# Attention followed by two Strassen-multiplied layers on one core: weight halves loaded in the order in which they are converted, one product with v moved to another bank, two matrix products placed between transposes and products with v

## The chip, the cores and the metric

The kernel runs on one core of one Trainium2 chip, in one launch. What is measured is the device time of one execution in microseconds (us). The profile is of one further execution of the same program; times below that carry a decimal point after the start of the span are read from it, counted from the span's first instruction.

## The reference

```python
def _attn_ref(q, k, v):                      # q, k, v: (2, 12, 448, 64)
    scores = scale * np.matmul(q, k.transpose(0, 1, 3, 2))
    scores = np.where(mask, -1000000000.0, scores)       # causal
    scores = scores - np.max(scores, axis=-1, keepdims=True)
    attn = np.exp(scores)
    attn = attn / (np.sum(attn, axis=-1, keepdims=True) + 1e-09)
    return np.matmul(attn, v).astype(np.float32)

def _moe_ref(x, w_in, w_out):                # x: (896, 768), w_in: (768, 2048)
    h = x @ w_in
    g = np.where(h >= 1, h, np.where(h <= -1, 0.0, (h + 1) ** 2 / 4.0))
    return (g @ w_out).astype(np.float32)

def _moe2_ref(x, w_gate, w_val, w_out, rms_g):           # w_gate, w_val: (768, 1536)
    xn = x / np.sqrt(np.mean(x * x, axis=-1, keepdims=True) + 1e-06) * rms_g
    g = xn @ w_gate
    return (g * (1.0 / (1.0 + np.exp(-g))) * (xn @ w_val) @ w_out).astype(np.float32)
```

The output is `_moe2_ref(_moe_ref(attention rearranged to 896 x 768))`. The weights are float64 in memory.

## The kernel before

**Attention.** The 24 pairs of batch and head are taken two heads at a time, in 12 groups (NG = 12, numbered 0 to 11). A group's scores are made in 112-row chunks (`scores`, L974 on TensorE), masked and reduced on VectorE (L982), turned into exponentials on ScalarE (L991), transposed on TensorE (`transposes`, L1012), copied out of PSUM by ScalarE (L1036) and VectorE (L1038), and multiplied with v on TensorE (`pv`, L1069). The product is divided by the row sums when VectorE copies it out (`xsplit`, L1080). The reciprocal row sums take a way of their own: VectorE (L1047), a DMA into a small row in DRAM (`factor`, L1049), two DMAs that spread it over partitions (`spread`, L1055). The table `PIPE` sets the order of these steps; it is run through once per group, with the steps of up to three groups in one pass. `pv(g)` belongs to the pass of group g+2. Every `pv` writes PSUM bank 7, so `pv(g)` cannot begin before `xsplit(g-1)` has read the bank.

**Layers.** The four matrix products (w_in, w_out, w_gate with w_val, w_out of the second layer) are done with Strassen's seven products on halves. The first, called in1 here, has 8 groups of columns with 7 products each; each product is 9 matmuls of 128x128 by 448 (L651), three k-blocks times three terms of a split into a high and a low part. A product is one unit of the list `units`. The first four units are product 1 of group 0, product 1 of group 1, product 2 of group 0 and product 2 of group 1. Products 1, 2 and 5 take tokens that early attention groups give; product 6, seventh in the list, is the first that takes those of the last three.

**Weights.** A weight matrix half (128 x 1536 words, float64) is loaded by `w_load` (L447, a DMA from SyncE) into one of two staging buffers and turned to float32 by `w_float`: a ScalarE pass over the high words (L479), a VectorE pass over the low words (L492; on some halves ScalarE, L490), a VectorE pass that joins them (L503). For the first two groups of in1 this happens during attention, in two half passes of 384 columns per matrix half. In `group`, the loads are asked for in the order src1, src2; the join asks for src2 first (`for i in (1, 0)`). Splits and sums on the results (L416, L424) go to ScalarE, VectorE or GpSimd.

**Order.** `Plan.run` places every operation on engines' time lines from a table of costs, with random trials from a fixed seed, and emits the instructions in the order found. Two of its inputs matter here: `tail`, the time that it assumes between a DMA's issue and its landing (5.0 us for a wide weight load), and `rel`, the earliest time of a load. A change of any of them can reorder everything behind. An engine's own instructions run in that order. TensorE's follow the order of the calls.

Of the kernel before, what the change touches and what calls it, by code (L numbers as in the profile page):

```python
# [27 lines left out]
PART = (0.1, 0.3, 1.0, 0.05)  # L28
GUARD = 0.0
BUSY = 7  # L30
QUIET = (5.0, 7.0)
JITTER = 0.5

# [66 lines left out]
class Plan:  # L100
# [104 lines left out]
    def place(self, peat, jitter, cross, same=0.06, guard=0.4):  # L205
# [23 lines left out]
        for i in order:  # L229
            best = None  # L230
            for e, (d, shared) in self.alts[i].items():
# [18 lines left out]
                else:  # L250
                    moved = True
                    while moved:
                        moved = False
                        for line, m in both:
# [4 lines left out]
                            while k < len(line) and line[k][0] < t + d + m:  # L259
                                t = max(t, line[k][1] + m)  # L260
                                moved = True
                                k += 1
                if e == "POOL" and best and any(peat[q] + lag - QUIET[0] < t + d and t < peat[q] + lag + QUIET[1]
                                                for q in self.quiet[1:]):
# [32 lines left out]
MM = 0.2035  # L297
GLEADS = ((24, 18, 16), (24, 18, 16), (24, 18, 16))
MOST1 = 2
AHEAD = 2  # L300
INTO = {2: 11, 21: 21, 22: 22, 3: 12}
FIRST = (21,)
# [8 lines left out]
def kernel(  # L311
# [43 lines left out]
    def ap(b, dtype=None):  # L355
        t = b.space.tile[:, b.off:b.off + b.n]
        return t if dtype is None else t.bitcast(dtype)
# [22 lines left out]
    def bank(i):  # L380
        return pst[:, i, :S]

    def bk(i):
        return BANK + i
# [23 lines left out]
    early = [True]  # L408
# [32 lines left out]
    def w_load(src, rel=0.0, most=3, area=None):  # L441
        if staged[0] >= min(staged[1], most):
            raise NoSpace
        st = SF.first(2 * NK * P if wide else NK * P, *((area,) if area else (SHORT, ())))
        staged[0] += 1
        if wide:
            op({"SP": 0.45}, lambda e: nc.sync.dma_start(out=ap(st, I32), in_=src.bitcast(I32)), [], [st],  # L447
               tail=5.0, rel=rel)
        else:
            op({"SP": 0.1}, lambda e: nc.sync.dma_start(out=ap(st), in_=src), [], [st], tail=4.6, rel=rel)  # L450
        return st
# [73 lines left out]
    def prep(stream, need, lead, fn, slow=False):  # L525

        def at(fn=fn, no=stage_no[0]):
            stage[0] = no
            fn()
        preps.append([need - lead, len(preps), need, at, stream, slow])  # L530
# [6 lines left out]
    def group(src1, src2, T, out, need, seeded, ps, rel=(0.0, 0.0), leads=(16, 10, 8)):  # L537
        st, wf, W = {}, {}, {}
        st_id = object()
        first = min(need.values())  # L540
        ld, lc, lm = leads

        def load(i, src):
            def f():
                st[i] = w_load(src, rel[i])
            return f

        def conv(i):
# [3 lines left out]
        def conv_half(i, h):  # L552
# [2 lines left out]
                    wf[i] = SF.first(NK * P, SHORT, ())  # L555
                w_float(st[i], False, wf[i], h)
            return f
        prep(st_id, first, ld, load(0, src1))
        prep(st_id, first, ld, load(1, src2))
        if ps:  # L560
            prep(st_id, first, lc, conv(1))
        else:
# [137 lines left out]
    def outer(n, load_src, G, out, order, plain=(), leads=(12, 8, 5, 20), apart={}):  # L700
# [61 lines left out]
        for p in phases:  # L762
# [6 lines left out]
            elif p == 6 and 22 in alone:  # L769
                line += seq[:AHEAD] + held_back + seq[AHEAD:]  # L770
            else:
# [10 lines left out]
        def load(i, src):  # L782
            def f():
                st[i] = w_load(src, most=MOST1 if plain else 2, area=area)
            return f
# [128 lines left out]
    NG = B * NP  # L914
# [32 lines left out]
    def seq(eng, dur, fn, r=(), w=(), **kw):  # L947
        plan.first.add(op({eng: dur}, lambda e: fn(), r, w, chain=eng, **kw))
# [14 lines left out]
    sbank, tbank, xbank = {}, {}, {}  # L963
# [95 lines left out]
    def pv(g):  # L1059
        i = g % 2  # L1060
        PT = PTs[i]
        xbank[g] = xb = 7
        parts = [(0, 1, 1, 3), (0, 11, 0, 1)] + [(kc, 4 * kc, kc, NCH - kc) for kc in range(1, NCH)]
        by_chunk = bank(xb).rearrange("p (i c) -> p c i", c=NCH)

        def fn():
            for n, (kc, blk, o, w) in enumerate(parts):
                for j in range(2):
                    nc.tensor.matmul(by_chunk[D * j:D * (j + 1), o:o + w], lhsT=Vr[i][:C, j, kc, :],  # L1069
                                     rhs=PT[:C, j, blk:blk + w],  # L1070
                                     start=(n == 0), stop=(n == len(parts) - 1), skip_group_check=True)
        seq("PE", 2.04, fn, [pts[i], vraw[i]], [bk(xb)], tail=0.1)
# [295 lines left out]
    def busy():  # L1368
        for _ in range(BUSY):
            nc.tensor.matmul(pst[:, 7, :P], lhsT=ap(ones), rhs=ap(ones), start=True, stop=True, skip_group_check=True)  # L1370
    seq("PE", 0.42 * BUSY, busy, [ones], [bk(7)])
    load_qk(1)
# [77 lines left out]
    def run_unit():  # L1450
        nonlocal nu
        now[0] = nu
        while later and later[0][0] <= nu:
            later.pop(0)[1]()
        emit_preps(nu, nu)
        units[nu]()
        nu += 1

    for g in range(NG + 2):
        early[0] = g < NG - 2  # L1460
        if g == NG:
            reserved.add(6)
        for what in PIPE:
            if what[0] == "R" and g == 0:
                load_qk(3)
            if 0 <= g + what[-1] < NG:
                if g == NG + 1 and what[0] == "PV":
                    run_unit()
                if g != 1 or what not in AHEAD1.values():
                    step(what[:-1], g + what[-1])  # L1470
                if g == 0 and what in AHEAD1:
                    step(AHEAD1[what][:-1], 1)
# [55 lines left out]
```

## Time and profile before

| | |
|---|---|
| median of 3 runs | 544.54 us (542.80, 544.54, 548.94) |
| the profiled execution | 545.35 us |
| its span, first to last instruction | 543.6 us, 1.75 us less |
| TensorE busy in the span | 531.3 us, 98% |
| VectorE, ScalarE, GpSimd | 472.6, 408.6, 152.1 us |
| granted TensorE clock | 1.000 (of 2.4 GHz) |

The span has three parts: attention up to about 88 us, the layers up to about 539 us, the last outputs. A time line row gives start, duration, engine, line, operation, tiles, shape and count, and in brackets how long the engine was idle just before and what ended it.

### The profile page before, as it was taken

Reading aid. Unit: us, or ns where it says so; the run is one execution under the profiler, and the core shown is the slowest. Engines: PE = TensorE matmul, PEld = TensorE weight load, DVE = VectorE, ACT = ScalarE, POOL = GpSimd, SP = SyncE. Lnnn points to the kernel's source line nnn. Section 1 sums busy time; section 2 is a strip of 40 time slices with the busy share of each in tenths; the row PEclk is TensorE's granted clock in tenths of the full one; section 3 lists DMA queues with packets and bytes.
Section 4 is the critical chain, followed back from the end, with each engine's and each line's share of the span. In section 5 each row is a group of like instructions: output and inputs, shape, how many; then the busy total and the mean of one; then the engine's idle time right before and its main releaser. Section 6 shows DMA issues by size and latency. Waiting matters only on the chain. (4 is left out here: it accounts for less than half of the span.)

```text
span 543.6 us, 8572 instructions
## 1 busy us (share of the span) xinstructions
PE 531.3 (98%) x2904; PEld 469.7 (86%) x2904; DVE 472.6 (87%) x939; ACT 408.6 (75%) x870; POOL 152.1 (28%) x148
## 2 busy tenths in 40 slices
PE   8999999999999999999999999999999999999996
PEld 6766767999999997999999889988999999999996
DVE  5898988999998899867579999989987878999992
ACT  6979888589988899855688854879787659667560
POOL 1176661620122311311011221342213003009360
PEclk9999999999999999999999999999999999999999
DMA  7783562334334765553063300655562533211012
GB/s 229 205 237 124 151 158 68 116 117 174 117 117 149 263 227 190 121 106 93 0 192 87 106 0 9 234 189 177 195 212 91 175 116 117 67 50 51 1 51 102
DMA packets 23372, 70.47 MB, mean 130 GB/s; under 512 B 5600, under 2 KB 13280, under 8 KB 23328
## 3 DMA queue, kind: packets, MB, share of 16 engines
q1 hardware_dynamic: 21456, 67.24, 38.1%
q0 software_dynamic: 1728, 2.62, 2.8%
q8 instruction: 23, 0.38, 0.3%
q14 instruction: 21, 0.17, 0.1%
q10 hardware_dynamic: 144, 0.06, 0.0%
HBM read 64.49 MB, written 2.80 MB: 124 GB/s over the span
## 5 line engine op out<-in xcount | busy, mean ns | idle before, releaser
L651 PE MATMUL ps<-sr 128*128 128x448 f32 x1260 | 259.8, 367 | 0.6 <-DVE sr L424 0.5
L651 PEld LDWEIGHTS ps<-sr 128*128 128x128 f32 x1260 | 235.8, 188 | 23.1 <-DVE sr L424 1.4
L746 PE MATMUL ps<-sr 128*128 128x448 f32 x918 | 188.4, 366 | 1.5 <-DVE sf L1124 0.8
L746 PEld LDWEIGHTS ps<-sr 128*128 128x128 f32 x918 | 171.8, 188 | 17.1 <-DVE sf L1124 1.2
L416 ACT CAST sr<-sf 128x384 fp32r<-128x384 f32 (+1 forms) x254 | 129.9, 537 | 58.5 <-DVE sf L424 25.5
L424 POOL TENSOR_TENSOR sr<-sf,sr 128x384 fp32r<-128x384 f32 (+1 forms) x65 | 89.1, 1383 | 228.7 <-ACT sr L416 207.2
L424 DVE TENSOR_TENSOR sr<-sf,sr 128x384 fp32r<-128x384 f32 (+1 forms) x207 | 126.2, 633 | 18.6 <-ACT sr L416 16.7
L424 DVE TENSOR_TENSOR sf<-ps,sf 128x448 f32<-128x448 f32 (+1 forms) x122 | 71.5, 599 | 13.9 <-PE ps L651 11.8
L479 ACT ACTIVATE sf<-sf 128x768 f32<-128x768 f32 (+1 forms) x72 | 63.2, 885 | 6.6 <-DMA sf<-in_w_in 4.0
L424 POOL TENSOR_TENSOR sf<-sf 128x448 f32<-128x448 f32 (+1 forms) x32 | 40.2, 1259 | 72.4 <-DVE sf L424 17.5
L416 ACT CAST sr<-ps 128x384 fp32r<-128x384 f32 (+1 forms) x82 | 38.4, 488 | 20.5 <-DVE ps L424 7.4
L991 ACT ACTIVATE sf<-ps,sf 112x336 f32<-112x336 f32 (+2 forms) x96 | 46.8, 505 | 9.0 <-DVE sf L982 7.5
L424 DVE TENSOR_TENSOR sr<-ps,sr 128x384 fp32r<-128x384 f32 (+1 forms) x82 | 44.8, 559 | 6.7 <-ACT sr L416 6.0
L424 DVE TENSOR_TENSOR sf<-sf 128x448 f32<-128x448 f32 (+1 forms) x73 | 46.3, 655 | 0.9 <-ACT sf L1187 0.5
L982 DVE CUSTOM_DVE_ANT_0 ps<-ps,sf 112x336 f32<-112x336 f32 (+2 forms) x96 | 41.1, 470 | 7.0 <-PE ps L974 6.1
L503 DVE SCALAR_TENSOR_TENSOR sf<-sf 128x768 int32<-128x768 int32 (+1 forms) x46 | 42.0, 918 | 1.7 <-ACT sf L490 0.6
L490 ACT ACTIVATE sf<-sf 128x768 int32<-128x768 uint8 x34 | 30.9, 912 | 0.0
L1012 PE MATMUL ps<-sf 112*112 112x112 f32 x240 | 27.0, 263 | 2.6 <-ACT sf L991 2.6
L503 DVE SCALAR_TENSOR_TENSOR ps<-sf 128x768 int32<-128x768 int32 x26 | 27.8, 1070 | 1.3 <-ACT sf L490 0.6
L416 ACT COPY ps<-ps 128x448 f32<-128x448 f32 x42 | 21.6, 519 | 9.2 <-PE ps L651 7.1
L1012 PEld LDWEIGHTS ps<-sf 112*112 112x112 f32 x240 | 22.9, 134 | 6.5 <-ACT sf L991 3.7
L974 PE MATMUL ps<-sf 64*112 64x336 f32 (+3 forms) x192 | 27.3, 413 | 1.0 <-DMA sf<-in_qT 0.5
(53 smaller groups left out, 348.9 us busy)
## 6 DMA issues: line engine op xcount, KB each, us to landing
sf<-in_w_out SPq DMA_DIRECT2D x28, 768.0 KB, 4.4
sf<-in_w_in SPq DMA_DIRECT2D x16, 768.0 KB, 5.1
sf<-in_w_gate SPq DMA_DIRECT2D x12, 768.0 KB, 4.3
sf<-in_w_val SPq DMA_DIRECT2D x12, 768.0 KB, 4.4
sf<-in_kT SPq DMA_DIRECT2D x12, 224.0 KB, 3.8
sf<-in_v SPq DMA_DIRECT2D x12, 224.0 KB, 3.6
sf<-row SPq DMA_DIRECT2D x24, 112.0 KB, 4.0
out_T<-sf SPq DMA_DIRECT2D x12, 224.0 KB, 1.9
```

The source lines that it names most:

```text
L416: op(alts, lambda e: nc.scalar.copy(dst, src) if e == "ACT" else nc.gpsimd.tensor_copy(dst, src), r, w, **kw)
L424: op(alts, lambda e: E[e].tensor_tensor(out=dst, in0=a, in1=b, op=alu), r, w, **kw)
L479: lambda e, words=words: nc.scalar.activation(words(1, F32), words(1, F32), ACTF.Prelu, scale=2.0 ** -112, alpha=-2.0 ** 32), [part], [top])
L490: nc.scalar.activation(words(0, I32), byte, ACTF.Copy, scale=7.49 / 255)
L503: nc.vector.scalar_tensor_tensor(out=out, in0=hi, scalar=3, in1=lo, op0=ALU.logical_shift_left, op1=ALU.bitwise_or)
L651: nc.tensor.matmul(bank(o), lhsT=ap(d.sub(x * HW + k * P, P)), rhs=ap(t.sub(y * S, S)), start=(begin and k == 0 and i == 0), stop=(k == HK ...
L746: nc.tensor.matmul(bank(o), lhsT=ap(a.sub(x * HW + d * P, P)), rhs=ap(t.sub(y * S, S)), start=((p == 1 or p > 7) and i0 == 0 and i == 0), ...
L974: nc.tensor.matmul(pst[:C, bs[j], o:o + (c + 1) * C], lhsT=ap(q)[r, c * C:(c + 1) * C], rhs=ap(k)[r, :(c + 1) * C], start=True, stop=True, ...
L982: seq("DVE", 0.145 + 0.00093 * (c + 1) * C, lambda t=t, c=c: nc.vector.tensor_tensor_reduce(out=t, in0=t, in1=ap(mask)[:C, S - (c + 1) * C ...
L991: seq("ACT", 0.23 + 0.0009 * w, lambda c=c, o=o, w=w: nc.scalar.activation(Pn[:C, j, poff[c]:poff[c] + w], pst[:C, sbank[n][j], o:o + w], ...
L1012: nc.tensor.transpose(pst[:C, bs[j][0], o:o + C], Pn[:C, j, poff[c] + kc * C:poff[c] + (kc + 1) * C], ap(ident)[:C, :C])
```

## The change

1. `load` gives the first load's earliest time to the half that is used first, and the two loads of a group that is not `ps` (the first two groups of in1) are asked for in the order src2, src1.
2. While `early[0]` is true (attention passes up to group 9), the plan assumes 8.5 us (WAIT0) in place of 5.0 us between issue and landing of a weight load.
3. `pv(NG - 2)`, the product with v of group 10, writes bank 6 (OWN) instead of bank 7.
4. One unit of in1 is run ahead of `pv(10)` and one ahead of `pv(11)` (FRONT); before, one was run ahead of `pv(11)` only.

```diff
+OWN = 6
+FRONT = (1, 1)
...
+WAIT0 = 8.5
...
-               tail=5.0, rel=rel)
+               tail=WAIT0 if early[0] else 5.0, rel=rel)
...
-                st[i] = w_load(src, rel[i])
+                st[i] = w_load(src, rel[i if ps else 1 - i])
...
-        prep(st_id, first, ld, load(0, src1))
-        prep(st_id, first, ld, load(1, src2))
+        for i, src in ((0, src1), (1, src2))[::1 if ps else -1]:
+            prep(st_id, first, ld, load(i, src))
...
-        xbank[g] = xb = 7
+        xbank[g] = xb = OWN if g == NG - 2 else 7
...
-                if g == NG + 1 and what[0] == "PV":
-                    run_unit()
+                if g >= NG and what[0] == "PV":
+                    for _ in range(FRONT[g - NG]):
+                        run_unit()
```

Lines of the changed kernel are numbered three higher from L447 on (L479 is L482, L651 is L654, L1069 is L1072), a few behind `pv` more. In the rows below, `sf` and `sr` are the two SBUF areas, `ps` is PSUM, `row_64` and `row_65` the two DRAM rows.

ScalarE early in attention (the pass from 15.5 us on), before: two half conversions (L479) stand in one pass.

```order
L1036 COPY sf<-ps 112x4x112 x2
L479 ACTIVATE sf<-sf 128x384
L991 ACTIVATE sf<-ps,sf 112x448 x2
L991 ACTIVATE sf<-ps,sf 112x336
L991 ACTIVATE sf<-ps,sf 112x112
L479 ACTIVATE sf<-sf 128x384
L991 ACTIVATE sf<-ps,sf 112x336
L991 ACTIVATE sf<-ps,sf 112x112
L991 ACTIVATE sf<-ps,sf 112x224
```

The same place in the changed kernel, up to the next conversion.

```order
L1039 COPY sf<-ps 112x4x112 x2
L482 ACTIVATE sf<-sf 128x384
L994 ACTIVATE sf<-ps,sf 112x448 x2
L994 ACTIVATE sf<-ps,sf 112x336
L994 ACTIVATE sf<-ps,sf 112x112
L994 ACTIVATE sf<-ps,sf 112x336
L994 ACTIVATE sf<-ps,sf 112x112
L994 ACTIVATE sf<-ps,sf 112x224
L1039 COPY sf<-ps 112x4x112
L994 ACTIVATE sf<-ps,sf 112x224
L1039 COPY sf<-ps 112x4x112 x2
L482 ACTIVATE sf<-sf 128x384
```

The second conversion moved to the next pass, and so did each of the six behind it; the eighth stands one pass behind the place of the last one before. VectorE's passes that join the words (L503) keep their places, one pass each.

TensorE at the end of attention, before: the 20 transposes of group 11, `pv(10)`, its last 4 transposes, one product of in1, the first matmuls of `pv(11)`.

```order
L1012 MATMUL ps<-sf 112x112 x20
L1069 MATMUL ps<-sf 64x3x112 x2
L1069 MATMUL ps<-sf 64x112 x2
L1069 MATMUL ps<-sf 64x3x112 x2
L1069 MATMUL ps<-sf 64x2x112 x2
L1069 MATMUL ps<-sf 64x112 x2
L1012 MATMUL ps<-sf 112x112 x4
L651 MATMUL ps<-sr 128x448 x9
L1069 MATMUL ps<-sf 64x3x112 x2
```

The same place in the changed kernel.

```order
L1015 MATMUL ps<-sf 112x112 x20
L654 MATMUL ps<-sr 128x448 x9
L1072 MATMUL ps<-sf 64x3x112 x2
L1072 MATMUL ps<-sf 64x112 x2
L1072 MATMUL ps<-sf 64x3x112 x2
L1072 MATMUL ps<-sf 64x2x112 x2
L1072 MATMUL ps<-sf 64x112 x2
L1015 MATMUL ps<-sf 112x112 x4
L654 MATMUL ps<-sr 128x448 x9
L1072 MATMUL ps<-sf 64x3x112 x2
```

A product of 9 matmuls now stands ahead of each of the last two products with v.

VectorE at the same place, before: `xsplit(9)`, two copies out of the transposes (L1038) with the reciprocal and three operations on tokens (L424) between them, `xsplit(10)`.

```order
L1080 TENSOR_TENSOR sf<-ps,sf 128x448
L1038 COPY sf<-ps 112x4x112
L1047 RECIPROCAL sf<-sf 112x8
L424 TENSOR_TENSOR sf<-sf 128x448 x2
L424 TENSOR_TENSOR sr<-sf,sr 128x448
L1038 COPY sf<-ps 112x2x2x112
L1080 TENSOR_TENSOR sf<-ps,sf 128x448
```

The same place in the changed kernel.

```order
L1083 TENSOR_TENSOR sf<-ps,sf 128x448
L1041 COPY sf<-ps 112x4x112
L1050 RECIPROCAL sf<-sf 112x8
L427 TENSOR_TENSOR sf<-sf 128x448 x2
L427 TENSOR_TENSOR sr<-sf,sr 128x448 x3
L1041 COPY sf<-ps 112x2x2x112
L1083 TENSOR_TENSOR sf<-ps,sf 128x448
```

Two more token operations stand ahead of the last copy of transposes, which `pv(11)` needs. On SyncE's queue the first load of group 2 of in1 moved about three passes forward, from behind the v load of group 10 to just ahead of the row write of an earlier group.

## Rows read from the trace of the kernel before

**Rows 1.** The page: busy time, share, instructions; 40 slices; TensorE's clock.
```profile
PE 531.3 (98%) x2904; PEld 469.7 (86%) x2904; DVE 472.6 (87%) x939; ACT 408.6 (75%) x870; POOL 152.1 (28%) x148
PE   8999999999999999999999999999999999999996
PEclk9999999999999999999999999999999999999999
```
**Rows 2.** Time line of PE, attention: first scores of a group, and one wait.
```profile
27.88 2.15 PE L974 MATMUL ps<-sf 64*112 64x448 f32 x16
...
34.06 2.15 PE L974 MATMUL ps<-sf 64*112 64x448 f32 x16
...
40.09 1.45 PE L1012 MATMUL ps<-sf 112*112 112x112 f32 x12 [1.32 <-ACT sf L991]
...
42.34 2.16 PE L974 MATMUL ps<-sf 64*112 64x448 f32 x16
...
49.08 2.39 PE L974 MATMUL ps<-sf 64*112 64x448 f32 x16 [0.49 <-DVE sf L1038]
...
55.62 2.39 PE L974 MATMUL ps<-sf 64*112 64x448 f32 x16
...
62.04 2.15 PE L974 MATMUL ps<-sf 64*112 64x448 f32 x16
...
68.22 2.15 PE L974 MATMUL ps<-sf 64*112 64x448 f32 x16
```
**Rows 3.** Time line of ACT: conversions of the first weights, one with a wait.
```profile
16.81 0.70 ACT L479 ACTIVATE sf<-sf 128x384 f32<-128x384 f32 x1
...
19.68 0.59 ACT L479 ACTIVATE sf<-sf 128x384 f32<-128x384 f32 x1
...
38.23 0.57 ACT L479 ACTIVATE sf<-sf 128x384 f32<-128x384 f32 x1 [2.67 <-DMA sf<-in_w_in]
```
**Rows 4.** Time line of SP's queue: weight loads three and four; spread of group 9.
```profile
23.32 0.46 SPq L447 DMA_DIRECT2D sf<-in_w_in  x1
...
29.57 0.46 SPq L447 DMA_DIRECT2D sf<-in_w_in  x1
...
73.25 0.35 SPq L447 DMA_DIRECT2D sf<-in_w_in  x1
73.65 1.09 SPq L1055 DMA_DIRECT2D sf<-row  x2
```
**Rows 5.** Line L447 up to 100 us: landing of the weight loads.
```profile
DMA to landing us min/median/max: 5.0/6.2/8.6
```
**Rows 6.** Time line of all engines, 38.5 to 48.5: two joins of words, one GpSimd operation.
```profile
38.79 0.56 DVE L503 SCALAR_TENSOR_TENSOR sf<-sf 128x384 int32<-128x384 int32 x1
...
46.93 1.14 POOL L424 TENSOR_TENSOR sr<-sf,sr 128x448 fp32r<-128x448 f32 x1
...
47.11 1.38 DVE L503 SCALAR_TENSOR_TENSOR sf<-sf 128x384 int32<-128x384 int32 x1
```
**Rows 7.** Time line, end of attention: pv(10), pv(11), their waits, and xsplit(9), xsplit(10).
```profile
80.58 0.62 DVE L1080 TENSOR_TENSOR sf<-ps,sf 128x448 f32<-128x448 f32 x1 [0.36 <-DMA sf<-row]
...
81.25 2.11 PE L1069 MATMUL ps<-sf 112*64 112x336 f32 x20 [0.61 <-DVE sf L1080]
...
83.66 2.10 PE L651 MATMUL ps<-sr 128*128 128x448 f32 x9
...
85.80 0.62 DVE L1080 TENSOR_TENSOR sf<-ps,sf 128x448 f32<-128x448 f32 x1 [1.24 <-DMA sf<-row]
...
86.53 2.11 PE L1069 MATMUL ps<-sf 112*64 112x336 f32 x20 [0.77 <-ACT sf L416]
```
**Rows 8.** Time line of PE behind 90 us: the three rows that have a wait.
```profile
207.41 73.18 PE L746 MATMUL ps<-sr 128*128 128x448 f32 x357 [0.79 <-DVE sf L1124]
...
299.98 5.32 PE L746 MATMUL ps<-sr 128*128 128x448 f32 x24 [0.65 <-ACT sr L416]
...
325.52 137.30 PE L651 MATMUL ps<-sr 128*128 128x448 f32 x671 [0.46 <-DVE sr L424]
```

## The prediction, made before the changed kernel was run

> **What bounds the kernel now.** First the page: TensorE is busy 531.3 of 543.6 us at the full granted clock, while VectorE has 87% and ScalarE 75% [rows 1]. No edit shortens a matmul or takes one away, so all that can be won is time in which TensorE stands: 12.3 us over the span, the ends included. So the question goes to TensorE's time line: where is it late, and what ended the wait?
>
> In attention, the first scores of a group (L974) mark one pass. Undisturbed passes take 6.18 us, with a weight conversion in them (27.88 to 34.06) or without (62.04 to 68.22) [rows 2]. Four passes in a row do not: 34.06 to 42.34 is 8.28, then 6.74, 6.54 and 6.42. Over 6.18 that is 2.10 + 0.56 + 0.36 + 0.24 = **3.26 us**. The listed waits show less of it (1.32 at 40.09, 0.49 at 49.08), since matmuls that trickle in with short gaps are drawn as longer ones: the distance between passes is the better measure.
>
> ScalarE's line says where this starts: a conversion begins at 38.23 after 2.67 us idle, ended by a DMA of w_in [rows 3]. So ScalarE asked at 35.56. The fourth weight load was issued at 29.57 [rows 4]; to 38.2 that is 8.6 us, the longest landing of those up to 100 us [rows 5]. ScalarE runs in order: the exponentials behind the conversion, and with them the transposes (1.32 us at 40.09), had to wait for weights that nobody needs before in1 begins at 83.66 [rows 7]. The passes behind are the echo. VectorE's join of weight words takes 0.56 us at 38.79, but 1.38 us at 47.11, where it overlaps a GpSimd operation begun at 46.93 [rows 6]; 0.49 us of wait for VectorE follows at 49.08.
>
> At the end of attention `pv(10)` stands 0.61 us for `xsplit(9)`, which itself waited for the spread row sums; `pv(11)` stands 0.77 us [rows 7]. The view names a ScalarE copy for the latter, but `pv(11)` must also wait for `xsplit(10)` to read bank 7; that ran from 85.80 to 86.42, 0.11 us before `pv(11)`, and had itself waited 1.24 us for its row. I take it to be the releaser. Behind 90 us three waits are left, 0.79 + 0.65 + 0.46 = 1.90 us [rows 8].
>
> **The change part by part.**
>
> *Order of loads, and WAIT0.* Either should end the wait alone. What group 1 needs first is now the third load, issued at 23.32 [rows 4]; with the longest landing it is there at 31.9. WAIT0 also moves the second and all later conversions one pass back (16.81 stays, the one at 19.68 goes to the next pass), so it is asked for near 35.56 + 6.18 = 41.7: 9.8 us of room. The other half, in place at 38.2, is used two passes after that. Price: the eight half conversions of about 0.6 us remain, one per pass; passes of that kind took 6.18. Before, ScalarE's conversions ran a pass ahead of VectorE's joins; now the fourth, near 16.81 + 3 x 6.18 = 35.35, is followed by its join at 38.79 in the same pass, 2.8 us behind its end. That cover is enough; were it gone, VectorE would stand, and at most the 0.6 us of a conversion would show in a pass. Term: **-3.26 us**, between -2.10 (the pass with the wait alone, if the echo has a cause of its own) and -3.26.
>
> The Trainium skill, page "DMA: Bandwidth & Descriptors", section "Anatomy of one DMA — SWDGE (gpsimd) path", gives a DMA about 2.0 us plus its bytes at 436 GB/s: an estimate of 3.8 us for this load of 768 KB. By it the fourth load would have been in place at 33.4, ScalarE would not have stood, and this edit would be worth nothing (545.35 - 1.38 = 543.97). The trace disagrees: 8.6 us and a wait of 2.67.
>
> *The load of group 2 that moved.* On SyncE's queue the weight load that stood just ahead of the spread of group 9 (73.25, then 73.65 [rows 4]) goes about three passes forward, ahead of a row write. The spread behind it cost `xsplit` 0.36 and `pv` 0.61 us at its old place. At the new one the same could happen once: 0 to +0.61. I take 0, since the third load stands four transfers ahead of the spread of a group, as this one will, and the pass from 27.88 to 34.06 has its 6.18 us. Its first VectorE pass now falls into the last pass of attention, where VectorE idled 0.36 us ahead of `xsplit(9)`; no more than a few tenths, on an engine that TensorE then does not wait for.
>
> *Bank 6 and the two products.* `pv(10)` no longer needs `xsplit(9)`: its 0.61 us go. `pv(11)` needs `xsplit(9)` instead of `xsplit(10)`, done 5 us before: its 0.77 us go. A product ahead of each costs nothing, since the same work leaves the row behind; each is 2.10 us of cover [rows 7]. What comes last then is the copy of the last transposes, which `pv(11)` reads: two more token operations stand ahead of it on VectorE, 2 x 0.62 (by `xsplit`, same shape) = 1.24 us, and 0.62 for itself, together 1.86, under the 2.10 of the product that now stands between. Should ScalarE's casts, which feed those operations, be late too, a part of 0.77 comes back: 0 to +0.5, I take 0. Behind `pv(11)` four products instead of five stand before product 6, which needs the last tokens: at 137.30 / 671 = 0.205 us a matmul [rows 8], 4 x 9 x 0.205 = 7.4 us for `xsplit` and three token operations of 0.62, 2.5 us and their handovers. Enough. Term: **-1.38 us**.
>
> *All that stands behind.* The plan is drawn anew, so that 450 us of order on VectorE, ScalarE and GpSimd differ in detail. The work is the same, and before it left TensorE 1.90 us of waits. A new draw can lose them or have as many again: -1.9 to +1.9. I take 0, having no row that favours either.
>
> **Sum.** 545.35 - 3.26 - 1.38 = 540.71 us against the profiled execution. That one lay 0.81 over the median of the three runs; from the median the same terms give 539.90. I take the middle, **540.3 us**, 0.8% under the median.
>
> **The rivals.**
>
> *The layers come out better.* The new draw loses the three waits: 540.3 - 1.9 = 538.4. For it: each is a hand-over at a change of stage, 0.46 to 0.79 us. Against: those changes of stage are still there. *Or worse*, by as much again, perhaps with a late row at the load's new place: 542.2 to 542.8.
>
> *The wait for weights is not in the plain runs.* Landings up to 100 us go from 5.0 to 8.6 us [rows 5]; one of 5.0 would have brought the fourth load by 34.6, ahead of 35.56, with no wait. If runs without the profiler are like that, then the load order and WAIT0 gain nothing there, and 544.54 - 1.38 = 543.2. For it: the lowest of the three runs, 542.80, lies where 545.35 - 3.26 = 542.1 would. Against: the median does not.
>
> *Slower.* The place is the layers, the mechanism VectorE and GpSimd meeting: the join at 47.11 took 0.82 us more beside a GpSimd operation, and TensorE stood 0.49 us behind it [rows 2, 6]. A redrawn order that has them meet, unseen by the plan once real times drift, pays that each time. It decides from 4.64 / 0.49, about ten such meetings that reach TensorE, and takes 21 to be 1% slower; then the time is 545 to 550. For it: the change redraws 450 us. Against: in the same 450 us of before only three waits reached TensorE at all.
> The Trainium skill, page "SBUF — State Buffer", section "Who interferes with whom", says that a VectorE instruction with two SBUF inputs and a GpSimd instruction that reads SBUF exclude each other for the whole instruction. The two joins agree, 1.38 against 0.56 us; by that rule a meeting can cost up to the whole 1.14 us of the GpSimd operation, and four or five would do.
>
> **How the numbers follow.** Forecast 0.50; better layers 0.17; worse layers 0.15; no wait in plain runs 0.12; slower 0.06. The range goes from 538.3 (better layers) to 543.2 (worse layers and the case without a wait); outside are the slow case and tails, under 2 in 10. About 1%, 5.4 us, is what a measurement of this kernel can tell from no change: below 539.1 lie the better layers and about a fifth of the forecast, 0.28; above 550 lies half of the slow case, 0.03; the rest, 0.69, is within.
>
> **What would show it.** In the changed profile: the conversions of L482 without a wait for w_in; first scores 6.18 us apart all through, so that those of 68.22 come at 65.0; joins at 0.56 us; `pv(10)` and `pv(11)` without a wait, the latter over by about 85.8 and both first products of in1 with it; before, `pv(11)` and the second of them, 2.05 and 1.84 us, took from 86.53 to 90.4. The forecast is wrong if a pass stays at 6.5 or more, if rows of sums land late near 55 to 65 us, if a product waits at 85 to 95 us for tokens, or if waits behind 90 us add up to over 4 us.

## The result, and the profile after

The changed kernel takes 548.02 us (median of 21 runs, 545.84 to 553.88), the kernel before 542.95 (21 runs, 541.07 to 548.94): ratio 1.0095, interval 1.0078 to 1.0111. It is slower by 5.1 us (4.2 to 6.0), not faster by 0.8%, and lies outside the range. The profiled execution of the changed kernel took 548.02 us too, its span 546.3.

The page of the changed kernel: busy time, TensorE in 40 slices, its clock.

```profile
PE 533.2 (98%) x2904; PEld 471.7 (86%) x2904; DVE 474.7 (87%) x937; ACT 408.8 (75%) x873; POOL 143.1 (26%) x147
...
PE   8999999999999998999999899999999999999996
...
PEclk9999999999999999999999799999999999999999
```

The sums hardly differ from [rows 1]; the slices do: TensorE has two new gaps, in the slices from 205 and from 300 us, and a lower clock in the second. Attention comes first. The time line of PE, first scores of a group (L977, L974 before), then the end of attention (L654 is a product of in1, L1072 a product with v):

```profile
33.58 2.15 PE L977 MATMUL ps<-sf 64*112 64x448 f32 x16
...
39.76 2.20 PE L977 MATMUL ps<-sf 64*112 64x448 f32 x16
...
46.54 2.39 PE L977 MATMUL ps<-sf 64*112 64x448 f32 x16 [0.48 <-DVE sf L1041]
...
53.13 2.38 PE L977 MATMUL ps<-sf 64*112 64x448 f32 x16
...
59.54 2.15 PE L977 MATMUL ps<-sf 64*112 64x448 f32 x16
...
77.94 2.09 PE L654 MATMUL ps<-sr 128*128 128x448 f32 x9
79.96 2.11 PE L1072 MATMUL ps<-sf 112*64 112x336 f32 x20
...
82.37 2.10 PE L654 MATMUL ps<-sr 128*128 128x448 f32 x9
84.39 2.11 PE L1072 MATMUL ps<-sf 112*64 112x336 f32 x20
86.44 3.91 PE L654 MATMUL ps<-sr 128*128 128x448 f32 x18
```

The pass of 8.28 us [rows 2] is gone (33.58 to 39.76 is 6.18), but the three behind it stay long: 6.78, 6.59, 6.41, against 6.74, 6.54 and 6.42 before. pv(10) and pv(11) have no wait. The third product of in1 starts at 86.44, where before it started near 90.5: 4.1 us, of which 0.45 is an earlier start of the first passes.

Then the gain goes. Both traces hold 2904 matmuls, so the k-th from the end can be compared. The 160 that ran from 181.25 to 215.46 us before, the end of in1 and the start of out1, took 34.2 us; now they take 38.6, from 176.41 to 214.96. The 160 around the norm (295.30 to 327.49 before) took 32.2 and now take 34.9. Behind 330 us both run alike, 2.4 us apart there and 2.7 at the end. The waits of PE behind attention, from its time line:

```profile
161.87 20.58 PE L654 MATMUL ps<-sr 128*128 128x448 f32 x99 [0.39 <-ACT ps L419]
...
183.11 3.91 PE L654 MATMUL ps<-sr 128*128 128x448 f32 x18 [0.66 <-DVE sf L427]
...
199.34 1.69 PE L749 MATMUL ps<-sr 128*128 128x448 f32 x7 [0.93 <-DVE sr L427]
...
205.95 2.70 PE L749 MATMUL ps<-sr 128*128 128x448 f32 x12 [0.91 <-DVE sf L1127]
...
214.04 66.18 PE L749 MATMUL ps<-sr 128*128 128x448 f32 x323 [0.48 <-DVE sr L427]
...
306.89 0.95 PE L1220 MATMUL ps<-sf 128*112 128x1 f32 x8 [1.21 <-DVE sf L427]
308.03 1.65 PE L1220 MATMUL ps<-sf 128*112 128x1 f32 x8 [0.20 <-ACT sf L1190]
```

Where the stretch had one wait of 0.79 before [rows 8] it now has six: 0.66 at the end of in1 and five at out1, 2.8 us in all, three of them shown. That is 2.6 us more; the rest of the 4.4 is matmuls that trickle in. All but two small ones (0.29 and 0.16, ScalarE) end with VectorE, and no wait of TensorE, VectorE or ScalarE in the stretch ends with GpSimd. VectorE's time line there, with GpSimd's (time line of all engines, rows of these two):

```profile
189.93 1.95 POOL L427 TENSOR_TENSOR sr<-sf,sr 128x448 fp32r<-128x448 f32 x1 [1.47 <-ACT sr L419]
190.78 1.52 DVE L495 TENSOR_SCALAR sf<-sf 128x768 int32<-128x768 int32 x1
...
194.14 0.55 DVE L495 TENSOR_SCALAR sf<-sf 128x768 int32<-128x768 int32 x1
...
196.92 1.41 POOL L427 TENSOR_TENSOR sr<-sf,sr 128x448 fp32r<-128x448 f32 x1 [5.04 <-ACT sr L419]
197.24 1.58 DVE L427 TENSOR_TENSOR sr<-sf,sr 128x448 fp32r<-128x448 f32 x1
...
202.28 2.26 POOL L427 TENSOR_TENSOR sr<-sf,sr 128x384 fp32r<-128x384 f32 x2 [3.95 <-ACT sr L419]
...
203.53 1.83 DVE L506 SCALAR_TENSOR_TENSOR sf<-sf 128x768 int32<-128x768 int32 x1
```

The same shift takes 0.55 us at 194.14 and 1.52 at 190.78, where GpSimd's subtraction began 0.85 us before it. Such an overlap of a VectorE operation with a GpSimd operation that reads SBUF, with the VectorE one over 0.25 us longer than others of its shape, is called a meeting from here on. From 182 to 206 us VectorE loses 4.2 us in five meetings (0.41, 0.96, 0.97, 0.97, 0.88 over the usual time of each shape); there it is full (9.8 of the 10 us from 190 on; 9.7 before). The kernel before lost 1.75 in two, at 188.85 and 203.68. Its time line, first a meeting and then a place without one:

```profile
188.51 1.44 POOL L424 TENSOR_TENSOR sr<-sf,sr 128x448 fp32r<-128x448 f32 x1 [1.35 <-ACT sr L416]
188.85 1.58 DVE L424 TENSOR_TENSOR sr<-sf,sr 128x448 fp32r<-128x448 f32 x1
...
194.84 0.62 DVE L424 TENSOR_TENSOR sr<-sf,sr 128x448 fp32r<-128x448 f32 x1
195.06 1.42 POOL L424 TENSOR_TENSOR sr<-sf,sr 128x448 fp32r<-128x448 f32 x1 [5.11 <-ACT sr L416]
195.48 1.02 DVE L424 TENSOR_TENSOR sr<-ps,sr 128x384 fp32r<-128x384 f32 x2
```

At 188.85 they meet. At 195.06 VectorE was already in its operation (0.62, undisturbed), and the two behind it, which take one operand from PSUM, run beside GpSimd at their usual 1.02.

### The profile page after: what moved, and what is told of

Its sections match the earlier page's. It is cut to its first block, busy times and chain, and to the rows that moved or that the text cites. A ratio compares the mean times of both kernels' runs of the same rounds, so it can differ in the third digit from the quotient of the medians.

```text
span 546.3 us, 8551 instructions
## 1 busy us (share of the span) xinstructions
PE 533.2 (98%) x2904; PEld 471.7 (86%) x2904; DVE 474.7 (87%) x937; ACT 408.8 (75%) x873; POOL 143.1 (26%) x147
## 4 chain that ended last, share of the span: by engine, by line
PE 74%; DVE 16%; ACT 6%; issue 2%; DMA 1%; POOL 0%; DVEq 0%; ACTq 0%; POOLq 0%
PE ps L654 36%; PE ps L749 25%; DVE sr L427 6%; DVE sf L427 5%; PE ps L1072 4%; PE ps L977 4%; PE ps L1015 4%; DVE ps L506 2%; ACT sr L419 2%; DMA sf<-in_w_out 1%; ACT sf L994 1%; DVE sf L506 1%; DVE sf L1127 1%; ACT sf L482 1%; PE ps L1373 1%
## 5 line engine op out<-in xcount | busy, mean ns | idle before, releaser
L654 PE MATMUL ps<-sr 128*128 128x448 f32 x1260 | 260.8, 368 | 1.3 <-DVE sf L427 0.7
L654 PEld LDWEIGHTS ps<-sr 128*128 128x128 f32 x1260 | 237.8, 190 | 22.5 <-DVE sf L427 1.0
L427 DVE TENSOR_TENSOR sr<-sf,sr 128x448 fp32r<-128x448 f32 (+1 forms) x207 | 130.0, 653 | 18.9 <-ACT sr L419 17.5
L427 POOL TENSOR_TENSOR sr<-sf,sr 128x384 fp32r<-128x384 f32 (+1 forms) x65 | 83.6, 1296 | 212.5 <-ACT sr L419 192.9
L482 ACT ACTIVATE sf<-sf 128x768 f32<-128x768 f32 (+1 forms) x72 | 62.9, 880 | 3.1 <-DMA sf<-in_w_val 1.8
L427 POOL TENSOR_TENSOR sf<-sf 128x448 f32<-128x448 f32 (+1 forms) x31 | 36.8, 1190 | 106.7 <-DVE sf L427 59.4
L994 ACT ACTIVATE sf<-ps,sf 112x336 f32<-112x336 f32 (+2 forms) x96 | 46.6, 503 | 8.9 <-DVE sf L985 8.0
L506 DVE SCALAR_TENSOR_TENSOR sf<-sf 128x768 int32<-128x768 int32 (+1 forms) x46 | 43.6, 949 | 2.0 <-ACT sf L482 0.8
L493 ACT ACTIVATE sf<-sf 128x768 int32<-128x768 uint8 x37 | 33.5, 906 | 0.0
L977 PE MATMUL ps<-sf 64*112 64x336 f32 (+3 forms) x192 | 27.0, 410 | 1.4 <-DMA sf<-in_qT 0.8
```

Of the source, the lines that this page charges most:

```text
L427: op(alts, lambda e: E[e].tensor_tensor(out=dst, in0=a, in1=b, op=alu), r, w, **kw)
L482: lambda e, words=words: nc.scalar.activation(words(1, F32), words(1, F32), ACTF.Prelu, scale=2.0 ** -112, alpha=-2.0 ** 32), [part], [top])
L493: nc.scalar.activation(words(0, I32), byte, ACTF.Copy, scale=7.49 / 255)
L506: nc.vector.scalar_tensor_tensor(out=out, in0=hi, scalar=3, in1=lo, op0=ALU.logical_shift_left, op1=ALU.bitwise_or)
L654: nc.tensor.matmul(bank(o), lhsT=ap(d.sub(x * HW + k * P, P)), rhs=ap(t.sub(y * S, S)), start=(begin and k == 0 and i == 0), stop=(k == HK ...
L977: nc.tensor.matmul(pst[:C, bs[j], o:o + (c + 1) * C], lhsT=ap(q)[r, c * C:(c + 1) * C], rhs=ap(k)[r, :(c + 1) * C], start=True, stop=True, ...
```

## The experiments

Theory 1: the layers were ordered anew, and the new order is worse wherever TensorE arrives. Theory 2: VectorE sets the pace at the start of out1, so whatever attention gives is waited out there. Theory 3 is in E3 that the wait and the clock at the norm cost the most, and from E7 on that a part of the change carries the loss by itself. Theory 4, formed after E1 to E4: the loss is VectorE standing beside GpSimd, where VectorE is full.

Several kernels keep an order that was planned for another. Their two last lines of the schedule read

```diff
-    plan.run()
+    for i in ORDER:
+        plan.fn[i](NAMES[ENG[i]])
```

with ORDER and ENG written out as tables at the end of the file.

The table holds what the verdicts rest on, worked out from each trace: the 160 matmuls at the start of out1 and the 160 at the norm (us), the excess of VectorE's operations within the former (us over the usual time of their shape, summed over the meetings, and how many they were), and the measured ratio to the kernel before.

```
                              out1 start   excess     norm    ratio and interval
before (profiled; again)      34.2; 34.1   1.75 (2)   32.2
changed (profiled; again)     38.6; 38.5   4.2 (5)    34.9    1.0095  1.0078-1.0111
E1  before, short attention   34.2         1.75 (2)   32.0    1.0030  0.9999-1.0061
E2  changed, 4.4 us late      37.6         4.2 (5)    33.5    1.0185  1.0142-1.0227
E3  changed, norm later       38.1         4.2 (5)    32.6    1.0087  1.0054-1.0120
E4  changed, middle as before 36.1         1.75 (2)   33.5    1.0142  1.0112-1.0173
E5  changed, zeros            34.3         0          33.4    0.9999  0.9975-1.0024
E6  E1 with zeros             34.1         1.75 (2)   32.2    1.0018  0.9992-1.0045
E7  changed, seed 7           36.6         2.4 (3)    32.0    1.0046  1.0019-1.0073
E8  before, seed 7            36.3         4.6 (5)    31.2    1.0031  0.9999-1.0063
E9  changed, six on VectorE   36.2         0          35.0    1.0058  1.0029-1.0087
E10 E9, norm later            36.7         0          32.5    1.0027  0.9998-1.0056
E11 loads alone               37.7         4.9 (5)    34.1    1.0058  1.0032-1.0083
E12 bank and products alone   36.7         4.1 (5)    30.8    1.0056  1.0027-1.0085
E14 before, seed 6            34.4         0.96 (1)   30.7    1.0003  0.9979-1.0026
E16 changed, seed 6           37.7         4.8 (6)    31.1    1.0045  1.0023-1.0068
```

**E1, a shorter attention before the old order.** Bank 6 for pv(10), and in the ORDER table ScalarE's conversion of 38.23 [rows 3] and the three behind it one pass later.

```diff
-        xbank[g] = xb = 7
+        xbank[g] = xb = 6 if g == NG - 2 else 7
```

> The kernel before with a smaller edit: pv(10) writes bank 6, and the ScalarE conversion that waited at 38.23 us and the three behind it stand one pass later in ScalarE's order. The rest of the order, that of all layers above all, is written out as it was before. It takes 2.1 to 3.3 us (the wait for w_in, with or without its echo) and 0.6 us (pv(10)) out of attention. Theory 1 (the changed kernel lost because its layers were ordered anew): the order is kept, so 2.7 to 3.9 us are kept to the end, ratio to before 0.993 to 0.995. Theory 2 (VectorE is full at the start of out1, so TensorE waits out there whatever attention gives): TensorE reaches out1 2.7 to 3.9 us earlier and at 280 us has at most 1 us left; ratio 0.998 to 1.001.

Ratio 1.003 (0.9999 to 1.0061): theory 1's number fails, and theory 2's (0.998 to 1.001) lies at the interval's edge. The time line of all engines shows where the gain went, not at out1 but at 101.74:

```profile
93.35 2.89 POOL L424 TENSOR_TENSOR sr<-sf,sr 128x448 fp32r<-128x448 f32 x2
93.79 2.93 DVE L424 TENSOR_TENSOR sr<-sf,sr 128x448 fp32r<-128x448 f32 x2
...
97.98 3.17 DVE L424 TENSOR_TENSOR sr<-sf,sr 128x448 fp32r<-128x448 f32 x3
...
98.20 1.26 POOL L424 TENSOR_TENSOR sf<-sf 128x384 f32<-128x384 f32 x1 [1.96 <-PE ps L651]
...
101.74 2.50 PE L651 MATMUL ps<-sr 128*128 128x448 f32 x11 [1.58 <-DVE sf L424]
```

TensorE was 1.6 us ahead of the kernel before at 98.6 and level with it at 115. The three subtractions of 97.98 take 1.55 where nothing meets them (E6). The order was the old one; only real times had shifted, and with them six meetings, 4.5 us, fell between 80 and 100 us, where before there were two, 1.1 us.

**E2, the changed kernel arriving late.**

```diff
         def fn():
+            for _ in range(19 * (g == NG - 1)):
+                nc.tensor.matmul(pst[:, xb, :P], lhsT=ap(ones), rhs=ap(ones), start=True, stop=True,
+                                 skip_group_check=True)
             for n, (kc, blk, o, w) in enumerate(parts):
```

> The changed kernel with 19 idle products of the 128 ones ahead of pv(11), about 4.4 us of TensorE (half of the 0.46 us that each took at the start of the program, at the lower clock), in an order that is else the same. It arrives at out1 when the kernel before does. Theory 1: the order of the layers costs what it costs, 548 + 4.4 = 552 us, ratio to before about 1.017. Theory 2: VectorE sets the pace from 187 to 220 us, the delay is taken up by the waits there: 548 to 549.5 us, ratio 1.009 to 1.012.

Ratio 1.0185: theory 1's number. TensorE reached the place at 181.83 us, 0.6 later than before, and still lost 3.4 us there. So the loss isn't a gain waited out. It weighs less than it looks: VectorE's last work of attention came 4.5 us later as well (91.78 for 87.29).

**E3, the norm later.** AT counts the products between the last of the layer and the norm's steps.

```diff
-    AT = ((3, 5, 3, 7), (1, 2, 2, 4))
+    AT = ((3, 5, 3, 7), (2, 3, 3, 5))
```

> The changed kernel in its own order, but TensorE's pieces of the second half's norm (both sums of squares, then the spread) stand one or two products later. Theory 3 (the wait of 1.21 us at 306.89 and the lower clock behind it cost 4 to 4.5 us, apart from the rest): no wait there, matmuls at 0.20 us instead of 0.37 from 309.6 to 316, the second layer's out starts 3 to 4.4 us earlier, 543.6 to 545 us, ratio 1.001 to 1.004. Rival (the wait moves to the spread, the clock falls all the same): at most 1 us, ratio 1.007 or more.

Split. In the trace the wait of 1.21 us gives way to one of 0.52, the granted clock stays at 1.00 (as in E10, below) and the stretch takes 32.6 instead of 34.9; the times, 1.0087, don't show it.

**E4, the middle as before.** The ORDER table between 100 and 250 us of the plan is the old kernel's, as far as reused buffers allow; some operations had to stand earlier than there.

> The changed kernel, in which the operations of the layers from the end of attention to the end of out1's first three quarters (100 to 250 us of the plan) stand in the order and on the engines of the kernel before; ahead of it and behind it its own. Theory 1: at least 2.5 of the 3.7 us lost from 187 to 220 us come back, 544 to 545.5 us, ratio 1.002 to 1.005. Theory 2: the waits at out1 stay, 547 to 548.5 us, ratio 1.007 to 1.011.

Neither: 1.0142. From 112 to 133 us TensorE lost 3.8 us at four waits for ScalarE and VectorE (0.89, 0.74, 1.34, 0.79) that neither kernel has; that they come from the operations moved ahead isn't shown. Only the stretch at out1 can be read: two meetings as in the old order, but 36.1 us, halfway. So the number of meetings alone doesn't set the loss.

**E5, GpSimd without reading.** Six subtractions are replaced.

```diff
-        op(alts, lambda e: E[e].tensor_tensor(out=dst, in0=a, in1=b, op=alu), r, w, **kw)
+        def fn(e):
+            if now_at[0] in CUT:
+                return nc.gpsimd.memset(dst.bitcast(F32), 0.0)
+            E[e].tensor_tensor(out=dst, in0=a, in1=b, op=alu)
+        op(alts, fn, r, w, **kw)
```

> The changed kernel in its own order, but the six subtractions that GpSimd has from 181.9 to 203.4 us write zeros instead, so that they read nothing (six low halves of operands are left out). Theory 4 (the loss at out1's start is VectorE standing beside GpSimd: five VectorE operations from 183 to 204 us take 0.4 to 1.0 us more than others of their shape, 4.0 in all, where VectorE is full): the excess goes, and the matmuls from 181.25 to 215.46 us of before, which took 34.2 there and 38.6 in the changed kernel, take 34.5 to 36; 544 to 545.5 us, ratio to before 1.002 to 1.005. Theory 1 in its plain form (VectorE's own order is worse there, GpSimd has no part): at most 1 us, ratio 1.007 or more.

Ratio 0.9999, 5.2 us below the changed kernel. Up to 181 us the two traces run alike to 0.04 us; then E5 takes 34.3 instead of 38.6. That is more than theory 4's 34.5 to 36. Another 1.5 us of the gain lies at the norm, which the edit doesn't touch: the wait there is the same, but the lower clock behind it lasted 3.4 us instead of 6.8. VectorE's time line, the same operations as above at 197.24 and 203.53:

```profile
194.79 0.62 DVE L430 TENSOR_TENSOR sr<-sf,sr 128x448 fp32r<-128x448 f32 x1
...
200.12 0.95 DVE L510 SCALAR_TENSOR_TENSOR sf<-sf 128x768 int32<-128x768 int32 x1
```

Theory 4 holds at out1's start, theory 1 in its plain form (VectorE's own order) falls. Since a zero also is there earlier than a difference, E9 was needed.

**E6, E1 without its meetings.** The edit of E5 in E1, for six operations from 80.1 to 99.4 us.

> The first experiment's kernel (attention 1.6 us shorter, lost again by a wait of 1.58 us for VectorE at 101.74), but the six subtractions and additions that GpSimd has from 80.1 to 99.4 us write zeros instead (parts of six operands are left out). Theory 4: VectorE loses the 4.5 us that six of its operations took too long from 80 to 100 us, the wait at 101.74 goes, and TensorE keeps 1.6 us and more to the end; ratio to before 0.995 to 0.998. Theory 2 (what attention gives is waited out in any case): a wait of the same size for VectorE or ScalarE there or at out1, ratio 1.000 to 1.003.

No meeting is left from 80 to 100 us and the wait at 101.74 is gone; TensorE keeps its lead through in1 and out1 (34.1). The ratio, 1.0018 (0.9992 to 1.0045), doesn't show the gain: the mechanism is in the trace, the time stays inconclusive. In the profile the lead of 1.15 us over the kernel before (E13) stands up to 216 us and is gone at 278; between the two lies a stretch in which TensorE runs 2% slower (last section).

**E7, E8, E14, E16, other draws.** Only the seed changes (to 6 in E14 and E16).

```diff
-SEED = 5
+SEED = 7
```

> The changed kernel with another seed of the planner (7 for 5), nothing else. Theories 1 and 4 (a draw of the layers' order decides): the excess of VectorE's operations from 180 to 205 us is another, and the time is 2 us or more from 548, more likely below: ratio to before 0.997 to 1.006. Rival (theory 3, a part of the change itself costs it): within 1 us of the changed kernel, ratio 1.008 to 1.011.

> The kernel before with another seed (7 for 5), nothing else. Theories 1 and 4, if the draw of the kernel before was a good one: more excess on VectorE from 80 to 110 or 180 to 205 us and 2 to 5 us more, ratio 1.004 to 1.009. Rival (draws cost nothing, the change does): ratio 0.998 to 1.002.

> The kernel before with seed 6. Theory 4: every draw but the first has three or four meetings of VectorE and GpSimd from 180 to 200 us; then 3 to 4 here too, 2 to 4 us lost at out1's start, ratio to before 1.002 to 1.008. If the draw of before is ordinary: one meeting, 0.998 to 1.001. Its attention shows a third time whether the wait for w_in comes.

> The changed kernel with seed 6, whose planned time is the shortest of its five seeds. Theory 4: its time goes with the meetings from 180 to 205 us; with three or four of them ratio 1.003 to 1.009, with one or none 0.997 to 1.002 and a version as fast as the kernel before or faster.

A draw is worth 2 to 3 us: the changed kernel goes from 1.0095 to 1.0046 and 1.0045, the one before from 1 to 1.0031 and 1.0003. In these draws the stretch at out1 goes with the meetings (34.1 to 34.4 us with one or two, 36.3 to 38.6 with three or more), but not in proportion: 2.4 us of excess give 36.6 (E7), 4.6 give 36.3 (E8), 4.2 give 38.6. Where meetings are few (E14) the time is that of before. E8 lies between its two expectations. E14's expectation fails: seed 6 has one meeting, so the old order was no rare luck. With seeds 5, 6 and 7 the kernel before has 2, 1 and 5 meetings, the changed one 5, 6 and 3, and with none of the three is the changed kernel the faster.

**E9, E10, the six on VectorE.** In the ENG table six operations change engine; E10 adds E3's edit.

```diff
-    (ENG of operations 1050, 1095, 1097, 1132, 1134, 1145: GpSimd)
+    (VectorE)
```

> The changed kernel in its own order, but the six subtractions that GpSimd has from 181.9 to 203.4 us run on VectorE, at the same place of the order; nothing is left out. Theory 4 counts VectorE's time: 4.0 us of standing beside GpSimd go, six operations of 0.53 us each from start to start come, 3.2 us; so 0.8 us are won at out1's start, with the earlier results at most 2: 546 to 547.5 us, ratio to before 1.006 to 1.009. Rival (GpSimd's results came late, and VectorE's fullness has no part): most of the 4.3 us comes back as with the zeros, ratio 1.000 to 1.003.

> As the kernel with the six subtractions on VectorE, and TensorE's pieces of the second half's norm one or two products later, as in the third experiment. It adds the 1.0 to 2.2 us that the third experiment's trace won there: ratio 1.002 to 1.006. Rival (what the norm gives is lost behind it, as the third experiment's times say): no better than without it, 1.006 to 1.009.

E9 wins 2.4 us at out1's start and 2.0 in time (1.0058, where the intervals of the two kernels overlap), more than the 0.8 that VectorE's bare account gives, at the limit of what theory 4 allowed, and not the rival's 1.000 to 1.003. With no meeting left, E9 stays 1.9 us above E5 in the stretch; its VectorE has the six operations more to do. A part of what E5 won may still be that zeros come earlier, though no wait of the changed kernel there ended with GpSimd; no run parts the two. E10 wins 2.5 us more at the norm, and in time 1.7 (the intervals overlap). TensorE and its clock at the norm, in windows (columns: busy PE, PEld, DVE, ACT, POOL; clock; DMA share; GB/s), of the changed kernel:

```profile
305.00:310.00 5.00, 3.59 (x21) 3.12 (x20) 4.89 (x11) 3.89 (x9) 0.00 (x0) 0.78 0.00 0
310.00:315.00 5.00, 5.00 (x16) 4.40 (x15) 3.82 (x11) 2.56 (x6) 0.00 (x0) 0.54 0.47 159
```

and of E10:

```profile
305.00:310.00 5.00, 5.00 (x35) 4.71 (x34) 4.58 (x11) 3.96 (x10) 0.00 (x0) 1.00 0.01 2
310.00:315.00 5.00, 4.48 (x26) 3.90 (x25) 4.70 (x12) 2.47 (x5) 0.00 (x0) 1.00 0.51 157
```

Behind the wait of 1.2 us the changed kernel's TensorE runs at a mean of 0.54, nearly all of it at the lower level of 1.2 GHz, and does 16 matmuls in 5 us; E10 has a wait of 0.52 us there, keeps 2.4 GHz and does 26.

**E11, E12, the parts.** E11 is the change without OWN and FRONT, E12 these alone.

> The kernel before with the order of the loads and WAIT0 alone (bank 7 for all products with v, one product of in1 ahead of the last). The wait of 2.67 us for w_in goes, passes of first scores as in the changed kernel, 2.0 to 2.1 us off attention (not the 3.26 of the prediction); the waits of pv(10) and pv(11), 1.4 us, stay. The layers are drawn anew. Theories 1 and 4: like any draw 0.998 to 1.008, with the excess on VectorE from 180 to 205 us going with it. Theory 3 (one part carries the loss): 1.008 or more here, or else with the bank and the products alone.

> The kernel before with bank 6 for pv(10) and the two products of in1 apart, but the loads in their old order and no WAIT0. The wait of 2.67 us for w_in stays, the 1.4 us of pv(10) and pv(11) go. The layers are drawn anew. Theories 1 and 4: like any draw 0.998 to 1.008, with the excess on VectorE from 180 to 205 us going with it. Theory 3: 1.008 or more here, if the loads alone are not.

1.0058 and 1.0056: neither part carries the loss alone, and each by itself is some 3 us slower. Both have five meetings at out1 and lose 3.5 and 2.5 us there. E11 has no wait for w_in and 44.5 us from the first scores of group 2 to those of group 9, as the changed kernel. E12 shows two waits for w_in, of 0.8 and 0.9 us, instead of one of 2.67. One expectation for E11 fails: with bank 7 and the old place of the products, its last two products with v have no wait either. Its time line of PE:

```profile
79.13 2.11 PE L1070 MATMUL ps<-sf 112*64 112x336 f32 x20
...
83.57 2.11 PE L1070 MATMUL ps<-sf 112*64 112x336 f32 x20
```

From the first scores of group 11 to the third product of in1 it takes 14.75 us, the changed kernel and E12 14.5, the kernel before 16.1 (15.9 in E13).

**E13, E15, both kernels again.** Nothing is changed.

> The kernel before, unchanged, profiled once more. If the wait of 2.67 us for w_in at 38.23 is a property of the program, as the prediction took it, it stands here again and passes of 8.2, 6.7, 6.5 and 6.4 us follow. If it belongs to single executions (third rival of the prediction, and what the kernel before with seed 7 showed: no wait, 44.4 us from the second group's first scores to the ninth's instead of 46.6), it is absent, and attention is 2.1 us shorter than in the profile of before.

> The changed kernel, unchanged, profiled once more. The four long VectorE operations from 182 to 204 us, and with them 3.5 to 4.4 us lost at out1's start, belong to the order and stand here again; the lower clock from 309 to 316 us belongs to single executions if it is absent (in two kernels with the same order of the norm and the same wait of 1.2 us it was), and then the stretch is about 1.5 us shorter.

E15 took 553.66 us, E13 543.71, one execution each. E15 shows the five waits at out1, the five long VectorE operations and the lower clock for 6.8 us again: the first two belong to the order, and the clock fell in both executions. E13 has the wait for w_in again, a little shorter; E8, in the time line of ACT, doesn't. E13:

```profile
38.30 0.60 ACT L479 ACTIVATE sf<-sf 128x384 f32<-128x384 f32 x1 [2.21 <-DMA sf<-in_w_in]
```

E8:

```profile
35.27 0.56 ACT L479 ACTIVATE sf<-sf 128x384 f32<-128x384 f32 x1
```

The longest landing of these loads was 8.6 us in the profile of before [rows 5], 8.2 in E13, 6.9 in E8. E14 waits 0.87 us, at another conversion (20.85). So both executions of the kernel before have the long wait, and the other orders with the old loads have less or none. From the first scores of group 2 to those of group 9, kernels with the old loads take 46.6, 46.1, 45.4, 45.4 and 44.4 us (before, E13, E14, E12, E8; mean 45.6), the eleven with the new ones 44.5 to 45.5 (mean 44.7).

## Why the prediction was wrong

**The step that failed** is "All that stands behind ... I take 0", with its bounds of -1.9 to +1.9 us. In the profiled pair the layers gave back 4.4 us around the start of out1 (the wait of 0.66 at the end of in1 included), 2.7 at the norm, and 0.39 earlier in in1. I had bounded what a new draw can cost by the waits that the one old draw showed. A sample of one bounds nothing: three draws of the kernel before spread over 1.7 us, three of the changed one over 2.7. The mechanism stood in the prediction as the last rival, slower by VectorE and GpSimd meeting, with 0.06, and the time lies in its 545 to 550 us. Its point of decision, ten meetings at 0.49 us each, was mis-sized: five, 4.2 us of VectorE's time, went with 4.4 us of TensorE's, because at the start of out1 VectorE is full; I had taken the price from attention, where it was busy 7.9 of 10 us (40 to 50 us). A price per meeting doesn't hold either: the two of the kernel before (1.75 us) cost nothing that shows (34.2 us; 34.3 in E5 without any), and five with 4.6 us cost E8 2.1. Two of the prediction's own signs came true: passes of 6.78 and 6.59 us, and waits behind 90 us of 5.2 in all. The three runs at hand also put the base 1.6 us too high, 544.54 for 542.95.

The Trainium skill, page "SBUF — State Buffer", section "Who interferes with whom", which the prediction cited, holds: a VectorE operation with two SBUF inputs behind a GpSimd one that reads SBUF waited for nearly all that was left of it (197.24: 0.97 of 1.09 us; 203.53: 0.88 of 1.01), those with an operand in PSUM didn't (195.48 before), and a GpSimd that only writes (E5) held up none. The same section says that VectorE in a two-port mode contends with GpSimd, and counts shifts of this kind (tensor_scalar) among what can enter one; the shift at 190.78, with one input and 1.52 instead of 0.55 us, fits, though no run shows the mode.

The 3.8 us that the prediction worked out from the Trainium skill, page "DMA: Bandwidth & Descriptors", section "Anatomy of one DMA — SWDGE (gpsimd) path", are that section's for a DMA issued through GpSimd. The weight loads go through SyncE's queue; up to 100 us they landed after 5.0 to 8.6 us before and 5.3 to 7.3 in the changed kernel.

**The term of -3.26 us** was mis-sized. The echo (1.16) is there without the wait: in all eighteen profiles three passes of 6.7 to 7.0, 6.5 to 6.6 and 6.4 us follow each other, and one join takes 1.3 to 1.4 us beside a GpSimd subtraction, as the one at 47.11 did before [rows 6]. In the changed kernel (time line of all engines, two rows):

```profile
44.39 1.14 POOL L427 TENSOR_TENSOR sr<-sf,sr 128x448 fp32r<-128x448 f32 x1
...
44.64 1.31 DVE L506 SCALAR_TENSOR_TENSOR sf<-sf 128x384 int32<-128x384 int32 x1
```

That this meeting makes the echo wasn't tried. The lower bound, -2.10, was right for the profiled pair (-2.05). With two profiles of each kernel the new loads give 1.3 us, over all the profiles of old and new loads 0.8. The rival "the wait for weights is not in the plain runs" stays open: both profiles of the kernel before have the wait, and no plain run shows its inside. What the order of the loads and WAIT0 do each by itself wasn't tried.

**The term of -1.38 us** held in size: both waits went, pv(11) was over at 86.5 with two products done. But it isn't the bank's and the products' alone: in E11, without them, the waits went too and all but 0.2 us was won. What took them there stays open. The load that moved costs a wait of 0.24 us for a row on VectorE at 66.05, which no product with v feels: nothing, as taken.

Added up over two profiles of each kernel, -1.3 and -1.5 in attention, +0.4 in in1, +4.4 around out1's start and +2.8 at the norm are 4.8 us, against 5.1 measured (4.2 to 6.0). Shown by taking it away are 4.3 of the 4.4 (E5; 2.4 in E9, which computes all) and, in the traces, 2.3 and 2.5 at the norm (E3, E10). Why each of the change's parts ends with more meetings than two of three old draws stays open: three seeds each can't tell a bias from luck. No kernel that computes all was faster than the one before; the nearest changed one is E10.

## What to carry to other kernels

Where an edit makes a planner draw the rest of the program anew, price the draw first: another seed of the unchanged kernel gives the spread, and a gain smaller than it can't be banked. A wait for a DMA in one profile is one landing; profile twice, and another draw too, before its length goes into a sum (2.67 and 2.21 us here, none with seed 7). Where VectorE is full, an operation on GpSimd that reads SBUF can be paid for on VectorE (0.3 to 1.0 us a meeting here), and keeping the two apart in planned time doesn't keep them apart in real time.

## What the runs showed of the hardware

TensorE's rate differs by 2% over long stretches at the same granted clock, and not in the same place in two executions of one program. Windows of the changed kernel, then of the same kernel again (E15):

```profile
360.00:460.00 100.00, 100.00 (x494) 92.47 (x493) 85.28 (x141) 77.99 (x142) 22.55 (x20) 1.00 0.49 170
```

```profile
360.00:460.00 100.00, 100.00 (x486) 90.83 (x485) 84.00 (x139) 77.25 (x139) 20.52 (x19) 1.00 0.47 166
```

TensorE waits for nothing in either: 494 matmuls in 100 us, 486 in the other. What makes the difference isn't shown. From 357 us to the end it costs E15 3.4 us. The profile of the kernel before has such a stretch from 88 to 200 us (340 matmuls from 110 to 180 us, 346 in E13), some 2 us that [rows 1 to 8] didn't show and that hid part of the loss in the profiled pair.

After one and the same wait of 1.2 us at the norm the granted clock differs: over the 10 us from about 1 us before the wait's end it was 0.66 in the changed kernel, E15 and E9 (37 or 38 matmuls), but 0.83 in E5, E2 and E4 (46 or 47). With shorter waits there, of 0.5 and 0.9 us (E3, E10; E7), 10 us around them held 56 matmuls at 1.00, and the clock stayed at 1.00 around a wait of 1.93 us at out1 (E8, 203.79) and one of 1.58 in in1 (E1, 101.74).
